# Six h buffers, spread transfers and a seven-product feature group in a gated attention kernel

## The chip, the cores and the metric

The kernel runs on one core of a Trainium2 chip. The metric is the device time of one execution in microseconds (us). The core has five engines that follow their own instruction streams in order and meet through semaphores: TensorE (PE, matmuls, with its weight loads listed as PEld), VectorE (DVE), ScalarE (ACT), GpSimd (POOL) and SyncE (SP), which here only issues transfers. Transfers are also issued from ACT and POOL. A letter q behind an engine's name in a row stands for its sequencer.

## The reference

One layer norm feeds two branches, whose product is added to the input. All data is float32; S = 2048 rows, D = 640, F = 1536.

```python
xn = _layernorm(x, axis=-1)
# A: attention over 8 keys at distance 0, 2, ..., 14; 32 heads of 20
qkv = (xn @ wqkv).reshape(B, S, 3, H, Dh)
idx = pos[:, None] - off[None, :]           # off = arange(8) * 2
logits = where(idx >= 0, einsum("bhsd,bhswd->bhsw", q, k[idx]) * scale, -1e9)
o = einsum("bhsw,bhswd->bhsd", softmax(logits), v[idx])
s = o @ wo
# B: bilinear GLU
h = (xn @ w_gate) * (xn @ w_up)
g = silu(h @ w_down)
out = x + s * g
```

## The kernel before

**Numbers.** Every matmul is done three times on parts: an operand is split into a rounded high part (ACT copy, `split`, line 109) and the low remainder (DVE or POOL subtraction, line 110), and high x high, high x low and low x high are added in PSUM. Splits are thus the constant side work: one ACT and one DVE or POOL instruction for each operand.

**Seven products.** Where it can, the kernel computes a 2x2 block product by seven block products (Strassen's scheme in Winograd's form). It needs sums of blocks on both sides: S1 to S4 (and d5) of the weights, made by `w_add` on POOL (line 1272) and split by `w_split`; T1 to T4 of the normalized, transposed x, kept in `xT` by four chunks of 512 rows. The T blocks of chunks 2 and 3 are made by `differences` (line 1190) during the qkv stage and stay on the chip. Those of chunks 0 and 1 are made early by `early_sums` and `early_high` (lines 583 and 596), stored to `t_scr` and `e_scr`, and loaded back by `load_t` and `load_e` from POOL's queue (lines 1179 and 1184).

**Stages**, in order of time:

1. Up to about 107 us: x is loaded, normalized and transposed; q, k, v of head group 0 and h of features 0 and 1 are computed between. For rows 8 to 15 the moments are spread over partitions by a small matmul (`spread`, line 340) behind a chain of small POOL operations (`scales`). `EARLY` (line 47) says how many of the eight `early_sums` of half 0 are issued ahead of the first `scales`.
2. To 274 us: the qkv projections of the other head groups (`qkv`, line 420). Results go through two or three staging tiles (`staged`: two halves of a slot and one "pk" tile) to `qkv_scr`. The attention runs beside it and goes on into the next stage: a generator (`attention`, line 461) that hands out DVE and POOL work as `advance` gives it credit per matmul. A unit is one head group and one parity of rows; DVE multiplies (527, 498) and reduces (534), POOL adds (504). `ahead` issues loads of q and k (part 0) and v (part 1) on SP.
3. 274 to 512 us: features 2 to 11, 128 each. `group(f, c0)` (line 1287) computes gate and up for two chunks by seven products in order 0, 5, 2, 1, 4, 3, 6, 54 matmuls in all. Products 0, 2, 1 and 4 are copied into an "h" buffer by ACT (`hold`, line 1295, tag "gh", five buffers); the sums `gate_b` (1298), `up_b` (1301), `gate_a` (1308) and the products `h_b` (1304), `up_a` (1311) work in these buffers, which are then stored to `h_scr` from SP. `up_b` and `h_b` stand on DVE for chunks 2 and 3 of features from `VEC` on, otherwise on POOL. Features from `F_TWO` = 3 to 10 take two such groups (chunks 2 and 3, then 0 and 1); feature 2 takes one, and `gate` and `up` (lines 1354 and 1363) for chunks 0 and 1 with 15 plain matmuls each; feature 11 takes one for chunks 0 and 1 and is plain for 2 and 3. The weights' gate part sits in the "pk" tile where a feature is two-way, and `load_wf` brings the next feature's weights.
4. 512 to 597 us: o times wo. Tiles of o come in pairs (`load_pair`), are turned and summed on DVE (`turn_pair`: lines 710 and 982 to 985), split by `hi_pair` on ACT and `lo_pair` on DVE (line 1012), and multiplied (`pair_product`, line 1033); sums and splits of w_down stand between (`wd_sums`, `wd_splits`). Six tiles follow singly.
5. To the end: h times w_down by seven products (line 896), silu, the gating with s and the output.

**Order.** Nothing is scheduled by a planner: each engine's stream is in the order in which the program issues. Two tables place side work behind a product: `places[second, n]` and `beside[f, second, n]`, where n counts the products of a group in issue order. `finish_piece` issues the last gating steps and the stores of a group behind the first product of the next one. Tiles with one tag share that tag's buffers: a new one waits until an old one has been read for the last time.

Of the kernel before, what the change touches and what calls it, by code (L numbers as in the profile page):

```python
# [19 lines left out]
P = 128  # L20
# [25 lines left out]
VEC = 3  # L46
EARLY = 3
# [9 lines left out]
def kernel(  # L57
# [17 lines left out]
    ps = ctx.enter_context(tc.tile_pool(name="ps", bufs=2, space=PSUM))  # L75
    dr = ctx.enter_context(tc.tile_pool(name="dr", bufs=1, space=DRAM))
# [298 lines left out]
    wide, now = [], [None]  # L375
# [44 lines left out]
    def qkv(m, r, i, runs=ALL_RUNS, at=None, act=None, bank=("q", 3)):  # L420
# [9 lines left out]
        if m or r:  # L430
            if not staged:
                y = slot([P, 2, 2 * 3 * CMAX], F32)
                staged.extend([y[:, 0], y[:, 1], st([P, 2 * 3 * CMAX], "pk", 1)])
# [27 lines left out]
    def attention():  # L461
# [45 lines left out]
        for n, u in enumerate(ORDER + [None]):  # L507
            if u is not None:
# [3 lines left out]
                ahead(n, (0, 1))  # L512
# [9 lines left out]
            for j in PAIRS:  # L522
                if u is not None:
                    ahead(n + 1, (0,))
# [20 lines left out]
            ahead(n + 1, (0, 1))  # L545
# [619 lines left out]
    F_TWO = 3  # L1165
# [121 lines left out]
    def group(f, c0=0, second=0):  # L1287
# [26 lines left out]
        if not second:  # L1314
# [65 lines left out]
    def next_sums(f):  # L1380
        w_split(f, "S", "R")
        w_sum.pop(f)
        if f < f1:
            load_wf(f + 1)

    def first_parts():
# [4 lines left out]
        yield  # L1391
        w_split(2, "G")
# [6 lines left out]
    for m, t in ((m, t) for m in range(1, len(MADE)) for t in range(DIL)):  # L1399
# [3 lines left out]
        for i in range(NE):  # L1403
# [9 lines left out]
            qkv(m, r, i)  # L1413
            if i == 1:
# [8 lines left out]
        elif (m, r) == (last, 1):  # L1423
            for k in range(2):
# [6 lines left out]
                   (f0, 1, 4): lambda: sums_wo(), (f0, 1, 5): lambda: split_wo(0, nc.vector),  # L1431
                   (f0, 1, 6): lambda: split_wo(1, nc.vector)})
# [16 lines left out]
    def load_late(n):  # L1449
        if n < 2:  # L1450
            load_t(n + 2)
        else:
            load_e(1, n - 2, n - 2)

    for f in range(2, f1):
        places.clear()
        if not two(f):
            places.update({(0, 3): sums("S1", "S2"), (0, 4): sums("S3", "d5", "S4")})
            if two(f + 1):
                places.update({(0, 0): lambda f: load_t(0), (0, 2): lambda f: load_t(1)})  # L1460
            group(f, 2)
            next_sums(f + 1)
            g0 = gate(f, 0)
            g1 = gate(f, 1)
            if two(f + 1):
                tw.pop("G")
            w_split(f + 1, "G")
# [207 lines left out]
```

## Time and profile before

| | us |
|---|---|
| median of 3 runs | 748.58 |
| lowest and highest | 748.15, 749.75 |
| the profiled execution, its time | 748.28 |
| the profiled execution, its span | 746.5 |
| PE busy | 735.4 |
| DVE busy | 612.2 |
| POOL busy | 462.6 |
| ACT busy | 302.5 |

The span runs from the first to the last instruction of the profiled execution. A row of a timeline has the start and the duration in us, the engine, the line, the operation, what is written and read by the program's names, shapes, and how many instructions are merged in the row; in brackets stands the idle time of the engine just before it and what ended it. A row of a wait list has who waited for whom, the total in us, the number of waits and the longest. Matmuls are pipelined, so the time between the starts of two rows, not their durations, says what a run of matmuls took.

### The profile page before, as it was taken

Reading aid. Unit: us, or ns where it says so; the run is one execution under the profiler, and the core shown is the slowest. Engines: PE = TensorE matmul, PEld = TensorE weight load, DVE = VectorE, ACT = ScalarE, POOL = GpSimd, SP = SyncE. Lnnn points to the kernel's source line nnn. Section 1 sums busy time; section 2 is a strip of 40 time slices with the busy share of each in tenths; the row PEclk is TensorE's granted clock in tenths of the full one; section 3 lists DMA queues with packets and bytes.
Section 4 is the critical chain, followed back from the end, with each engine's and each line's share of the span. In section 5 each row is a group of like instructions: output and inputs, shape, how many; then the busy total and the mean of one; then the engine's idle time right before and its main releaser. Section 6 shows DMA issues by size and latency. Waiting matters only on the chain. (4 is left out here: it accounts for less than half of the span.)

```text
span 746.5 us, 11102 instructions
## 1 busy us (share of the span) xinstructions
PE 735.4 (99%) x4054; PEld 669.0 (90%) x4054; DVE 612.2 (82%) x720; ACT 302.5 (41%) x577; POOL 462.6 (62%) x389
## 2 busy tenths in 40 slices
PE   8999999999999999999999999999999999999997
PEld 6989989988999998778887888887899999999997
DVE  7666998699697887998999999667998777777775
ACT  5658413323332332233223322335556564444442
POOL 6169929787688878888879989877559800000000
PEclk9999999999999999999999999999999999999999
DMA  9465672947446548856165424268567655555534
GB/s 316 170 202 200 236 224 87 299 157 239 127 152 197 190 128 232 274 161 207 55 159 149 115 82 110 72 178 204 167 177 212 228 220 191 191 191 191 191 106 141
DMA packets 103493, 132.98 MB, mean 178 GB/s; under 512 B 22696, under 2 KB 74404, under 8 KB 103438
## 3 DMA queue, kind: packets, MB, share of 16 engines
q1 hardware_dynamic: 84686, 112.77, 48.4%
q10 hardware_dynamic: 17600, 14.26, 5.9%
q0 software_dynamic: 1152, 5.24, 2.2%
q8 instruction: 32, 0.52, 0.3%
q14 instruction: 23, 0.19, 0.1%
HBM read 83.58 MB, written 47.81 MB: 176 GB/s over the span
## 5 line engine op out<-in xcount | busy, mean ns | idle before, releaser
L504 POOL TENSOR_TENSOR o<-o,t 128x960 f32<-128x960 f32 (+1 forms) x69 | 139.6, 2024 | 19.1 <-DVE t L498 17.6
L498 DVE TENSOR_TENSOR t<-e,kv 128x960 f32<-128x960 f32 (+1 forms) x96 | 99.4, 1037 | 24.8 <-POOL o L504 24.7
L527 DVE TENSOR_TENSOR t<-q,kv 128x1920 f32<-128x1920 f32 (+1 forms) x48 | 92.4, 1925 | 4.3 <-DMA kv<-qkv_scr 4.2
L534 DVE TENSOR_REDUCE lg<-t 128x96 f32<-128x1920 f32 (+1 forms) x48 | 92.3, 1922 | 0.2
L428 PE MATMUL q<-s,xc 128*128 128x360 f32 (+1 forms) x450 | 83.1, 334 | 0.6 <-DVE lg L266 0.5
L110 POOL TENSOR_TENSOR s<-wraw,s 128x384 fp32r<-128x384 f32 (+6 forms) x58 | 69.6, 1210 | 19.9 <-ACT s L109 19.9
L428 PEld LDWEIGHTS q<-s,xc 128*128 128x128 f32 x450 | 74.9, 188 | 4.8 <-DVE lg L266 0.8
L1295 ACT ACTIVATE gh<-g 128x512 f32<-128x512 f32 x54 | 32.2, 597 | 115.8 <-PE g L1328 97.8
L428 PE MATMUL u<-s,xc 128*128 128x360 f32 (+1 forms) x360 | 65.8, 334 | 0.0
L428 PEld LDWEIGHTS u<-s,xc 128*128 128x128 f32 x360 | 60.3, 188 | 2.3
L428 PE MATMUL g<-s,xc 128*128 128x360 f32 (+1 forms) x330 | 61.5, 337 | 0.0
L428 PEld LDWEIGHTS g<-s,xc 128*128 128x128 f32 x330 | 55.7, 188 | 2.6
L1328 PE MATMUL u<-xc,s 128*128 128x512 f32 x216 | 55.3, 391 | 0.9 <-ACT gh L1295 0.9
L896 PE MATMUL q<-xc,s 128*128 128x320 f32 x342 | 55.5, 309 | 0.0
L1328 PE MATMUL g<-s,s 128*128 128x512 f32 x216 | 55.0, 390 | 0.0
L896 PEld LDWEIGHTS q<-xc,s 128*128 128x128 f32 x342 | 51.5, 188 | 0.0
L1328 PEld LDWEIGHTS u<-xc,s 128*128 128x128 f32 x216 | 40.3, 188 | 10.5 <-ACT gh L1295 2.0
L1328 PEld LDWEIGHTS g<-s,s 128*128 128x128 f32 x216 | 40.5, 188 | 8.6 <-ACT gh L1295 0.2
L109 ACT ACTIVATE s<-wraw 128x384 fp32r<-128x384 f32 (+6 forms) x59 | 33.5, 587 | 29.5 <-PE g L1328 9.0
L504 POOL TENSOR_TENSOR o<-t 128x960 f32<-128x960 f32 (+1 forms) x12 | 24.4, 2032 | 31.8 <-DVE t L498 25.2
L1328 PE MATMUL g<-xc,s 128*128 128x512 f32 x168 | 41.5, 391 | 1.3 <-ACT gh L1295 1.3
L119 PE MATMUL g<-xc,s 128*128 128x512 f32 (+1 forms) x180 | 40.1, 373 | 0.0
(367 smaller groups left out, 1566.5 us busy)
## 6 DMA issues: line engine op xcount, KB each, us to landing
h_scr<-gh SPq DMA_DIRECT2D x48, 256.0 KB, 2.6
wraw<-in_wgu SPq DMA_DIRECT2D x11, 640.0 KB, 4.4
kv<-qkv_scr SPq DMA_DIRECT2D x14, 480.0 KB, 5.9
qkv_scr<-s ACTq DMA_DIRECT2D x18, 360.0 KB, 4.4
t<-h_scr SPq DMA_DIRECT2D x8, 768.0 KB, 7.1
kv<-qkv_scr SPq DMA_DIRECT2D x14, 367.5 KB, 6.6
s_scr<-gh SPq DMA_DIRECT2D x16, 320.0 KB, 4.2
gh<-s_scr SPq DMA_DIRECT2D x16, 320.0 KB, 3.5
```

The lines of the kernel that those rows point to most:

```text
L109: nc.scalar.activation(hi, raw, AF.Copy)
L110: eng.tensor_sub(lo, raw, hi.bitcast(F32))
L119: nc.tensor.matmul(acc, a, b, start=first and n == 0, stop=last and n == len(runs) - 1)
L428: nc.tensor.matmul(p, xT[(r * NE + i) // TPC][a][:, k, t0:t0 + P], wq[m][b][k], start=n == 0, stop=n == len(runs) - 1, skip_group_check=ac ...
L498: nc.vector.tensor_mul(t.rearrange("p (n d) -> p n d", d=DH), e[:, :, w].unsqueeze(2).to_broadcast([P, NE * nh, DH]), v)
L504: return NE * c * cost, lambda: eng.tensor_add(y, z, t)
L527: nc.vector.tensor_mul(t, q, k)
L534: nc.vector.tensor_reduce(out=lg[:, :, j:j + 2].rearrange("p n a -> p a n"), in_=t.rearrange("p a (n d) -> p a n d", d=DH), op=ALU.add, ax ...
L896: nc.tensor.matmul(p, y[:, i, k], wd_t[name][k][:, l], start=new and r == 0, stop=r == len(runs) - 1, skip_group_check=True)
L1295: nc.scalar.activation(kept[j], b["ACACABA"[j]], AF.Copy)
L1328: nc.tensor.matmul(y, w, x, start=j in (0, 1, 5) and r == 0, stop=r == len(runs) - 1, skip_group_check=True)
```

## The change

It has these parts. `F_TWO` becomes 2: feature 2 takes two groups of seven products, so its gate weights go to the "pk" tile (the staging of the last qkv products gives that tile up), its up weights shrink to three blocks, the sums of feature 3's weights take the places that later features use, and all loads of T and e blocks of chunks 0 and 1 come a feature earlier. `VEC` becomes 2 with it. `EARLY` becomes 1. The "gh" tag gets a pool of its own with six buffers, which is closed ahead of the pairs and followed by one of five. `load_wf` moves from the start of a group behind its first product. In `attention` the loads of v move from the end of the unit before to the third key of their own unit, and those of q and k behind that. The stores of q, k, v of head group 0 go from ACT's queue to SP's. On the way to the o pairs, `split_wo(0)`, `split_wo(1)` and `turn_pair(0)` come one or two products later, and `turn_pair(2)` goes from between the last gate and up to behind product 5 of pair 0.

```diff
-VEC = 3
-EARLY = 3
+VEC = 2
+EARLY = 1
...
+    halfway = ExitStack()
+    gh_pool = [halfway.enter_context(tc.tile_pool(name="six", bufs=1)), 6]
...
-        return sb.tile(shape, dt, tag=tag, bufs=bufs, name=f"{tag}_{cnt[0]}")
+        pool = sb
+        if tag == "gh":
+            pool, bufs = gh_pool
+        return pool.tile(shape, dt, tag=tag, bufs=bufs, name=f"{tag}_{cnt[0]}")
...
-                    nc.scalar.dma_start(scr[2 * g + r][:, :, i - 1:i + 1, :], y[:, k])
+                    (nc.scalar if m else nc.sync).dma_start(scr[2 * g + r][:, :, i - 1:i + 1, :], y[:, k])
...
-                ahead(n, (0, 1))
+                ahead(n, (0, 1) if late_unit else (0,))
...
             for j in PAIRS:
                 if u is not None:
-                    ahead(n + 1, (0,))
+                    if j == 2:
+                        ahead(n, (1,))
+                    elif j > 2:
+                        ahead(n + 1, (0,))
...
-            ahead(n + 1, (0, 1))
+            ahead(n + 1, (0,))
...
-    F_TWO = 3
+    F_TWO = 2
...
             wf_raw.pop(f)
-            if f < f1 and f + 1 not in wf_raw:
-                load_wf(f + 1)
...
+            if (second, n) == (0, 0) and f < f1 and f + 1 not in wf_raw:
+                load_wf(f + 1)
             advance(PACE * len(runs) * (GROUP_RATE if two(f) else 0.184))
...
         w_split(2, "S")
-        yield
-        w_split(2, "G")
         yield
...
             qkv(m, r, i)
+            if m == last and n == NT - 7:
+                staged[:] = [y for y in staged if y is not stage_pk[-1]]
+            elif m == last and n == NT - 5:
+                load_t(0)
+            elif m == last and n == NT - 3:
+                w_split(2, "G")
...
-                   (f0, 1, 4): lambda: sums_wo(), (f0, 1, 5): lambda: split_wo(0, nc.vector),
-                   (f0, 1, 6): lambda: split_wo(1, nc.vector)})
+                   (f0, 1, 4): lambda: sums_wo(), (f0, 1, 6): lambda: split_wo(0, nc.vector)})
...
     def load_late(n):
-        if n < 2:
-            load_t(n + 2)
+        if n == 0:
+            load_t(1)
+            load_t(2)
+        elif n == 1:
+            load_t(3)
         else:
-            load_e(1, n - 2, n - 2)
+            load_e(1, 0, 0)
+            load_e(1, 1, 1)
...
         places.update(two_places)
         if f == F_TWO:
-            places.update({(0, n): lambda f, n=n: load_late(n) for n in range(4)})
+            for n in range(3):
+                places[0, n] = lambda f, n=n: load_late(n)
         group(f, 2)
         group(f, 0, 1)
     places.clear()
-    beside.update({(f1, 0, 0): lambda: (turn_pair(0), load_pair(1)), (f1, 0, 4): lambda: (hi_pair(0, 0), lo_pair(0, 0)),
+    beside.update({(f1, 0, 0): lambda: split_wo(1, nc.vector),
+                   (f1, 0, 2): lambda: (turn_pair(0), load_pair(1)), (f1, 0, 4): lambda: (hi_pair(0, 0), lo_pair(0, 0)),
...
     g3 = gate(f1, 3)
-    turn_pair(2)
     up(f1, 3, g3)
...
     pair_k.append(st([P, 3, HALF], "o", 1))
+    halfway.close()
+    gh_pool[:] = [ctx.enter_context(tc.tile_pool(name="five", bufs=1)), 5]
...
         if p == 0:
             load_pair(4)
+            turn_pair(2)
```

The branch of the loop for a feature that is not two-way (its `places`, `next_sums`, `gate` and `up` for chunks 0 and 1) falls away.

More of the change, by code (lines that the diff above doesn't have):

```diff
@@ L1378, in up @@
         advance(PACE * 2.8)
[L1380 to L1384, printed above, removed]
     def first_parts():
@@ L1449, in load_late @@
     def load_late(n):
-        if n < 2:
-            load_t(n + 2)
-        else:
-            load_e(1, n - 2, n - 2)
+        if n == 0:
[3 more added lines that the diff above has]
+            load_t(3)
+        else:
+            load_e(1, 0, 0)
+            load_e(1, 1, 1)
     for f in range(2, f1):
         places.clear()
[L1457 to L1467, printed above, removed]
-            up(f, 0, g0)
-            up(f, 1, g1)
-            if two(f + 1):
-                tw.pop("U")
-            continue
         places.update(two_places)
         if f == F_TWO:
-            places.update({(0, n): lambda f, n=n: load_late(n) for n in range(4)})
+            for n in range(3):
+                places[0, n] = lambda f, n=n: load_late(n)
         group(f, 2)
```

5 lines of the change are left out of this document (3 added, 2 removed).

## The prediction

> **What bounds the kernel now.** I read the page first, then the list of who waited for whom with TensorE (PE) as the one that waits, with the total, the number of waits and the longest, then a table of busy time by stretch.
>
> ```profile
> span 746.5 us, 11102 instructions
> PE 735.4 (99%) x4054; PEld 669.0 (90%) x4054; DVE 612.2 (82%) x720; ACT 302.5 (41%) x577; POOL 462.6 (62%) x389
> ```
>
> ```profile
> PE g L1328 <- ACT gh L1295: 1.3, 2, 0.9
> PE e L340 <- POOL lg L334: 1.0, 1, 1.0
> PE u L1328 <- ACT gh L1295: 0.9, 2, 0.6
> PE e L1033 <- DVE xc L1012: 0.8, 1, 0.8
> ```
>
> ```profile
> 273.90:299.70 25.80, 25.80 (x116) 21.40 (x115) 20.13 (x24) 8.53 (x15) 22.60 (x21) 1.00 0.82 230
> 299.70:472.60 172.90, 171.17 (x749) 139.74 (x749) 162.22 (x160) 54.36 (x91) 147.69 (x114) 1.00 0.49 140
> 525.80:566.00 40.20, 39.10 (x262) 38.28 (x261) 37.09 (x60) 24.60 (x54) 22.68 (x20) 1.00 0.58 163
> ```
>
> The columns of the table are the stretch, its length, then PE, weight loads, DVE, ACT, POOL, the granted clock, DMA share and GB/s. PE is busy in all but 11.1 us of the span and is the bound in every stage, so only two things shorten the kernel: fewer matmuls, or fewer of its holes. The waits list names the holes one by one, and each has a place in the change. The table gives the warning: in the feature groups DVE is busy 162.22 of 172.90 us, in the output pairs 37.09 of 40.20. It is the next bound, close behind.
>
> **Part 1, feature group 2: fewer matmuls.**
>
> ```profile
> 273.90 1.52 PE L1328 MATMUL g<-xc,s 128*128 128x512 f32 x6
> ...
> 286.14 3.56 PE L119 MATMUL g<-xc,s 128*128 128x512 f32 x15
> ...
> 299.74 1.90 PE L1328 MATMUL g<-xc,pk 128*128 128x512 f32 x6
> 301.48 2.21 PE L1328 MATMUL q<-xc,pk 128*128 128x512 f32 x9
> ...
> 299.29 1.56 POOL L110 TENSOR_TENSOR pk<-wraw,pk 128x640 fp32r<-128x640 f32 x1
> ```
>
> From 273.90 to 286.14 chunks 2 and 3 go by seven products: 54 matmuls in 12.24 us, 0.2267 each. From 286.14 to 299.74 chunks 0 and 1 go by plain gate and up: 60 matmuls in 13.60. The second becomes a second 54, so **-1.36 us**, six matmuls by 0.2267. Then the first product of group 3 takes 1.74 us where six take 1.36: the gate weights were split too late (POOL at 299.29, the product at 299.74). With group 2 as a two-way group these weights are split five products ahead, as in the later groups: **-0.38**.
>
> What it adds. POOL gets the up sum and h product of chunks 0 and 1 and gives those of chunks 2 and 3 to DVE; DVE also gets the two gate sums and a product in place of two plain products. The nearest row for the sums and the product on DVE is this one:
>
> ```profile
> L1304 DVE TENSOR_TENSOR gh<-gh,gh x8: 679/1000/2370, 314.8 to 490.1; 128x512 f32<-128x512 f32 x8
> ```
>
> Two more on DVE are 1.4 to 4.7 us, the two gate sums about as much as the two products that go. The stretch of group 2 has 5.67 us of idle DVE to take it, so I cost it at nothing; with that cover gone it would be the same 1.4 to 4.7 us at most. The Trainium skill (SBUF — State Buffer, "Who interferes with whom") has a rule that speaks against this step: a VectorE instruction with two SBUF inputs and a GpSimd instruction that reads SBUF exclude each other for a whole instruction. The spread from 679 to 2370 ns agrees; by the rule DVE falls behind whenever POOL is full, which is the first rival below.
>
> The T blocks, the sums of x for chunks 0 and 1, must also be in a group earlier. Block 0 is issued five qkv products before the group, 1 and 2 behind its first product, 3 behind the second, the two e blocks behind the third, all on POOL.
>
> ```profile
> 279.93 0.76 POOL L1182 DMA_DIRECT2D s<-t_scr  x1
> ...
> DMA to landing us min/median/max: 8.8/10.6/11.7
> ```
>
> At 279.93 POOL stood at the place where blocks 1 and 2 will now be issued. They are needed 15 matmuls into the second half, at 286.14 + 3.40 = 289.54. With the shortest landing block 1 is there at 288.7 and block 2 just behind: no stall. With the longest it lands at 291.6 and block 2, 768 KB at the 230 GB/s of the stretch, 3.4 us later: at most 5.5 us at that product, and 6.7 when the e blocks, 2.3 us each behind block 3, hold the last product too. Ends 0 and 6.7; I take **+0.6**, near the short end, because the key loads of the attention that ran beside them move away and block 0 is already in. The Trainium skill (DMA: Bandwidth & Descriptors, "Anatomy of one DMA — SWDGE (gpsimd) path") puts such a transfer at 2.0 us plus bytes over 436e3 per us, an estimate of 3.8 us for 768 KB. The trace has 8.8 to 11.7, and the trace decides; by the page's figure this term would be 0.
>
> The gate split of group 2 (1.56 us on POOL) and the issue of block 0 (0.76) now stand among the attention's last sums of the qkv stage, ahead of the R and U splits that products three and four want: ends 0 and 2.3. I take 0: the same split leaves POOL's queue a few products earlier, in front of the same sums, and U shrinks from five blocks to three. The q, k, v staging does without its third tile for the last products; each of the two others still has a pair of products in which its store can land: 0.
>
> **Part 2, EARLY 3 to 1.**
>
> ```profile
> 44.84 3.59 PE L119 MATMUL g<-xc,s 128*128 128x512 f32 x15
> 49.46 0.41 PE L340 MATMUL e<-lg,lg 128*128 128x32 f32 x2 [1.03 <-POOL lg L334]
> ...
> 43.79 2.55 POOL L593 TENSOR_TENSOR kv<-xc 128x512 f32<-128x512 f32 x2 [17.92 <-DVE xc L370]
> ...
> 47.55 0.21 POOL L278 TENSOR_TENSOR lg<-lg 128x4 f32<-128x4 f32 x1
> ...
> 45.02 0.17 DVE L277 RECIPROCAL lg<-lg 128x4 f32<-128x4 f32 x1
> ```
>
> The product of 15 ends at 44.84 + 15 x 0.2267 = 48.24; the spread starts at 49.46, so the hole is 1.22. It waits for the scales chain on POOL, which starts at 47.55 behind three early sums and ends just before 49.46. With one early sum ahead POOL is free at 45.1 and the reciprocal is there at 45.2: the chain starts 2.3 us earlier. **-1.22**. Two sums move behind the second scales and end later; their stores and, on SP, the stores of unit 1's q, k and v queue behind them. What waits for those is the attention, by the loads that come next, not a product: 0.
>
> **Part 3, six buffers of h and the spread transfers.**
>
> ```profile
> 320.86 2.20 PE L1328 MATMUL u<-xc,s 128*128 128x512 f32 x9
> 323.53 2.35 PE L1328 MATMUL g<-xc,s 128*128 128x512 f32 x9 [0.47 <-ACT gh L1295]
> ...
> 332.52 1.52 PE L1328 MATMUL g<-s,s 128*128 128x512 f32 x6
> 334.34 2.35 PE L1328 MATMUL u<-xc,s 128*128 128x512 f32 x9 [0.30 <-ACT gh L1295]
> ...
> 395.82 2.20 PE L1328 MATMUL u<-xc,s 128*128 128x512 f32 x9
> 398.90 2.34 PE L1328 MATMUL g<-xc,s 128*128 128x512 f32 x9 [0.87 <-ACT gh L1295]
> ...
> 505.89 1.52 PE L1328 MATMUL g<-s,s 128*128 128x512 f32 x6
> 508.01 2.34 PE L1328 MATMUL u<-xc,s 128*128 128x512 f32 x9 [0.60 <-ACT gh L1295]
> ```
>
> ```profile
> ACT gh L1295 <- DMA h_scr<-gh: 12.3, 4, 6.9
> ```
>
> Against 0.2267 each the four holes are 0.63, 0.46, 1.04 and 0.76: 2.89. Each ends when ACT's copy of a product into an h buffer is done, and that copy had waited for a buffer: the one before it was still being stored. A sixth buffer gives every copy one store more of time. The stores also start sooner: they no longer stand on SP behind the next group's weight load nor, at a unit's end, behind loads of k and v that wait for DVE; the weight load comes a product later, four ahead of the sums that read it, and the v load two steps into its own unit, a unit ahead of its use: 0 each. What is late next is DVE's gating, which the sixth buffer covers too. Between keeping all four holes (0) and losing them all I take **-2.89**.
>
> **Part 4, o pairs.**
>
> ```profile
> 531.10 1.48 PE L1033 MATMUL g<-s,kv 128*128 128x320 f32 x9
> 532.42 0.75 PE L1033 MATMUL e<-s,xc 128*128 128x320 f32 x4
> 533.96 0.56 PE L1033 MATMUL e<-s,xc 128*128 128x320 f32 x2 [0.78 <-DVE xc L1012]
> 534.75 1.15 PE L1033 MATMUL q<-xc,kv 128*128 128x320 f32 x6 [0.23 <-DVE gh L1042]
> ...
> 536.18 1.04 PE L1033 MATMUL u<-xc,s 128*128 128x320 f32 x6
> 537.30 1.14 PE L1033 MATMUL e<-xc,s 128*128 128x320 f32 x6
> ...
> 527.73 1.56 DVE L710 STREAM_TRANSPOSE s<-s 128x640 f32<-128x640 f32 x2
> ...
> 532.41 1.50 DVE L1012 TENSOR_TENSOR xc<-s,xc 128x640 fp32r<-128x640 f32 x1
> ```
>
> Here a matmul takes (532.42 - 531.10) / 9 = 0.147. From 532.42 to 534.75 six stand: 1.45 too long. Nine to 536.18 are 0.11 too long, six to 537.30 0.24. Together 1.80. The low part that PE waits for (532.41) stands on DVE behind the turning of pair 2 from 527.73 on, some 3.2 us. That step moves behind product 5 of pair 0, where nothing waits for it before pair 2. So the low part comes 3.2 us sooner and the holes go: **-1.80**. But DVE, full to 37.09 of 40.20, must do the step between two pairs: ends 0 and 1.80 again. The five h buffers of the second half also start there, over the six, and DVE's first sum into one may wait for the last h store. I take **+0.4** for both, near the low end, because the pairs' stretch has 3.1 us of idle DVE, about one turning. The same order ahead of group 11 (gate sums before the turning of pair 0) shortens the last hole of part 3 and is counted there.
>
> **Sum.** -1.36 - 0.38 + 0.6 - 1.22 - 2.89 - 1.80 + 0.4 = -6.65. The profiled execution took 748.28 us, its span 746.5, so it would be 741.63. The median of the runs shown, 748.58, is 0.30 above it: **741.9**.
>
> **The rivals.** *DVE becomes the bound.* For it: 162.22 of 172.90 busy, and PE gives back some 3 us of that stretch while up to 4.7 come in. Against: 10.7 us of it are idle, and six buffers let gating lag. The holes of part 3 then come back as waits for gating, two thirds of them: 741.9 + 1.9 = 743.8.
>
> *The hole of the pairs only moves.* Pair 2 is turned between the high parts of pair 1 and its own, and PE waits at pair 2 as it did at pair 1: the 1.80 comes back, 743.7, or twice that if pair 3 follows late, 745.5. Against: the low part of pair 2 is needed some 8 us later than that of pair 1.
>
> *The T blocks come late, and the kernel is slower.* POOL is busy 22.60 of 25.80 in this stretch, and the gate split and block 0 stand ahead. If POOL reaches blocks 1 and 2 three us later than 279.93 and landing takes the longest, 11.7, block 2 lands at 298.0 and the second e block near 306, against 296.3 where the last product wants it: 9.7 us of hole, 741.9 - 0.6 + 9.7 = 751. It turns the sign once block 2 lands later than about 297. For it: longest landing seen under just such traffic. Against: less runs beside them now, and block 0 is out of their way.
>
> *The sixth buffer does nothing,* because the copies wait for stores that come no earlier: part 3 falls out, 744.8. The wait row, which names the store itself, speaks against it.
>
> **How the numbers follow.** The forecast has 0.58, DVE 0.13, the moved hole 0.09, the idle sixth buffer 0.07, the late blocks 0.13, of which 0.09 above 750.1 and 0.04 near no change. The range starts at 739.8: without the two added terms the sum gives 740.9, and after a hole nine matmuls take 2.35 us where they take 2.20 at 320.86, 0.15 more for each of seven holes. It ends at 746.5 and leaves out little but the late blocks. A measurement of this kernel can tell about 0.2%, 1.5 us, from no change. Below 747.1 lie the first four cases, 0.87, of which I take 0.03 off for two of them at once: faster 0.84, within 0.07, slower 0.09.
>
> **What would show it.** Right: 54 matmuls in the second half of group 2; the spread for rows 8 to 11 starts as its gate product ends; no wait of PE for ACT's gh copies; none for L1012 in the first pairs. Wrong: PE waiting for a T block at the third product of group 2's second half, copies still waiting for h stores, or DVE with no idle time between 300 and 470 and PE holes behind its gate sums.

## The result and the profile after

The changed kernel takes 745.4 us (median of 5 runs, 744.77 to 745.68). The kernel before, run beside it, took 748.95 us (748.15 to 750.33). The ratio is 0.9948, with a 95% interval of 0.9933 to 0.9962. So the kernel is faster, and inside the range of 739.8 to 746.5, but it gained about half of the 6.65 us of the sum: 3.55 us by the medians, 2.88 between the two profiled executions.

The profiled execution took 745.40 us against 748.28 before. Here are the line of its page on the engines, and the list of what PE waited for from the start of group 2 to the first products of the last stage. Lines of the code are five to nine higher than before: 1335 is the product of a group, 1304 the copy into an h buffer, 1313 the product h. In the pairs 1042 is the product, 1045 ACT's copy of a product, 1048, 1051 and 1053 are the sums on DVE and 1021 the low parts. 510 is a sum of the attention, 115 a split's subtraction, 905 a product of the last stage.

```profile
PE 734.1 (99%) x4048; PEld 668.4 (90%) x4048; DVE 620.4 (83%) x723; ACT 303.0 (41%) x579; POOL 464.0 (62%) x389
```

```profile
PE u L1335 <- POOL s L115: 1.1, 1, 1.1
PE q L1042 <- DVE gh L1051: 0.9, 1, 0.9
PE e L1042 <- DVE gh L1051: 0.4, 1, 0.4
PE e L1042 <- ACT o L1045: 0.4, 1, 0.4
PE u L905 <- ACT s L864: 0.2, 1, 0.2
PE g L1335 <- ACT gh L1304: 0.2, 1, 0.2
```

Six matmuls are gone, as forecast, and PE is busy 1.3 us less. The waits for ACT's copies, 2.2 us before, are down to 0.2. But two names stand here that did not stand there: a weight split on POOL, and sums on DVE in the pairs. The same shows in the table by stretch (columns as before: stretch, length, PE, weight loads, DVE, ACT, POOL, granted clock, DMA share, GB/s):

```profile
272.40:296.90 24.50, 24.50 (x110) 20.33 (x109) 23.27 (x30) 8.87 (x16) 23.10 (x23) 1.00 0.99 295
296.90:468.80 171.90, 171.75 (x755) 141.21 (x755) 162.14 (x155) 55.68 (x93) 147.14 (x112) 1.00 0.44 129
468.80:493.30 24.50, 23.40 (x104) 19.03 (x103) 16.15 (x17) 6.77 (x12) 20.20 (x15) 1.00 0.46 134
521.17:562.96 41.79, 39.85 (x262) 38.27 (x261) 38.69 (x60) 24.53 (x54) 23.55 (x21) 1.00 0.59 160
```

In group 2 the added sums have used up most of DVE's idle time, from 5.67 to 1.23 us, and PE has no hole there. Features 3 to 9 run almost without a hole (171.75 of 171.90). Feature 10 loses 1.1 us. The pairs, 40.17 us long before, take 41.79, and DVE is busy 38.69 us in them, against 37.06 before.

A ledger, read from the starts of PE's rows in the two profiled executions:

| stretch | before | after | measured | forecast |
|---|---|---|---|---|
| to the first product of group 2 | 273.90 | 272.47 | -1.43 | -1.22 |
| group 2 | 25.84 | 24.48 | -1.36 | -1.36, +0.6 for the T blocks |
| group 3 to the first plain product of feature 11 | 212.49 | 210.51 | -1.98 | -0.38 and -2.89 |
| plain products of feature 11 | 13.60 | 13.71 | +0.11 | 0 |
| the pairs | 40.17 | 41.79 | +1.62 | -1.80 and +0.4 |
| single tiles of o | 27.72 | 27.73 | +0.01 | 0 |
| last stage, to the last matmul | 148.07 | 148.43 | +0.36 | 0 |
| sum | | | -2.67 | -6.65 |

**Where parts 1 and 2 gained.** The second half of group 2 is now 54 matmuls, and nothing in it waits. The columns of a timeline are start, duration, engine and line, tiles and count.

```profile
284.71 1.52 PE L1335 MATMUL g<-xc,pk 128*128 128x512 f32 x6
...
288.11 1.52 PE L1335 MATMUL g<-s,s 128*128 128x512 f32 x6
...
296.95 1.52 PE L1335 MATMUL g<-xc,pk 128*128 128x512 f32 x6
```

```profile
L1191 POOL DMA_DIRECT2D s<-t_scr x4: 537/557/758, 264.1 to 279.1; - x4
...
DMA to landing us min/median/max: 5.6/8.6/11.0
```

The second block of rows sums up the T blocks' loads. They land in 5.6 to 11.0 us. Block 2 is the one that counts: it landed at 287.97, and the product that reads it began at 288.11. The margin is narrow. In the run with five buffers below the same load landed at 288.16, and the third matmul of that product, due at 288.10, began at 288.20.

```profile
44.70 3.59 PE L124 MATMUL g<-xc,s 128*128 128x512 f32 x15
48.13 0.30 PE L345 MATMUL e<-lg,lg 128*128 128x32 f32 x2
```

The spread's small matmuls now start as the product of 15 ends (44.70 + 15 x 0.2267 = 48.10); the wait of 1.03 us for POOL is gone.

**What is new at 477 us.** Two timelines, of PE and POOL:

```profile
475.44 0.61 PE L1335 MATMUL u<-xc,s 128*128 128x512 f32 x2
477.16 0.50 PE L1335 MATMUL u<-xc,s 128*128 128x512 f32 x1 [1.10 <-POOL s L115]
```

```profile
471.73 2.25 POOL L510 TENSOR_TENSOR o<-o,t 128x960 f32<-128x960 f32 x1
473.94 1.29 POOL L1310 TENSOR_TENSOR gh<-gh,gh 128x512 f32<-128x512 f32 x1
475.19 1.91 POOL L115 TENSOR_TENSOR s<-wraw,s 128x384 fp32r<-128x384 f32 x1
```

The low parts of feature 10's up weights (475.19) stand on POOL behind a sum of the last attention unit and an up sum. They end at 477.10, and the third matmul of the product that reads them starts then, 1.27 us late, with 0.11 more on the next matmul. DVE had been idle for 2.21 us, up to 474.02.

**What is new in the pairs.** PE and DVE at the first pair:

```profile
527.77 1.04 PE L1042 MATMUL e<-s,xc 128*128 128x320 f32 x6
529.67 1.14 PE L1042 MATMUL q<-xc,kv 128*128 128x320 f32 x6 [0.86 <-DVE gh L1051]
```

```profile
526.14 0.81 DVE L1021 TENSOR_TENSOR xc<-s,xc 128x640 fp32r<-128x640 f32 x1
528.73 0.49 DVE L1048 TENSOR_TENSOR gh<-o,u 128x320 f32<-128x320 f32 x1 [1.77 <-POOL kv L115]
529.13 0.48 DVE L1051 TENSOR_TENSOR gh<-o,q 128x320 f32<-128x320 f32 x1
```

DVE sits idle for 1.77 us before its first sum into one of the five new buffers (528.73), and the second sum, which PE needs, stands behind it. The view names a POOL split as the releaser, which ended at 528.54. The last store of h, issued at 525.89, landed at 528.44, so either could be it. Further on DVE has 0.09 us of idle time at two places and no more up to 559 us, and a hole of 0.3 to 0.5 us, with 0.1 on the next matmul, stands in each pair.

Which DVE rows grew? Mostly the four low parts of 128x768. Here is the second of them, before and after:

```profile
540.26 0.95 DVE L1012 TENSOR_TENSOR kv<-s,kv 128x768 fp32r<-128x768 f32 x1
```

```profile
536.67 1.46 DVE L1021 TENSOR_TENSOR kv<-s,kv 128x768 fp32r<-128x768 f32 x1
```

Before, all four began as a POOL split ended or ahead of one, and took 0.94 to 0.95 us. After, three of the four begin 0.24 to 0.42 us into a POOL split of 0.88 us, and take 1.27 to 1.46. That is 1.3 of the 1.6 us by which DVE is busier.

### The profile page after: what moved, and what is told of

It reads as the page before. It is cut to its first block, busy times and chain, and to the rows that moved or that the text cites. A ratio compares the mean times of both kernels' runs of the same rounds, so it can differ in the third digit from the quotient of the medians.

```text
span 743.6 us, 11095 instructions
## 1 busy us (share of the span) xinstructions
PE 734.1 (99%) x4048; PEld 668.4 (90%) x4048; DVE 620.4 (83%) x723; ACT 303.0 (41%) x579; POOL 464.0 (62%) x389
## 5 line engine op out<-in xcount | busy, mean ns | idle before, releaser
L1304 ACT ACTIVATE gh<-g 128x512 f32<-128x512 f32 x57 | 34.1, 598 | 113.2 <-PE g L1335 110.1
L1335 PE MATMUL u<-xc,s 128*128 128x512 f32 x228 | 58.4, 390 | 1.1 <-POOL s L115 1.1
L1335 PE MATMUL g<-s,s 128*128 128x512 f32 x228 | 58.1, 390 | 0.0
L1335 PEld LDWEIGHTS u<-xc,s 128*128 128x128 f32 x228 | 42.8, 188 | 10.9 <-POOL s L115 1.9
L1335 PEld LDWEIGHTS g<-s,s 128*128 128x128 f32 x228 | 42.7, 188 | 9.2 <-ACT gh L1304 0.4
L1335 PE MATMUL q<-xc,pk 128*128 128x512 f32 x171 | 41.8, 389 | 0.0
```

The source lines that it names most:

```text
L1304: nc.scalar.activation(kept[j], b["ACACABA"[j]], AF.Copy)
L1335: nc.tensor.matmul(y, w, x, start=j in (0, 1, 5) and r == 0, stop=r == len(runs) - 1, skip_group_check=True)
```

## The experiments

All runs change the kernel after, unless said otherwise. "Groups to end" is the time from the first product of group 2 to the end of the last matmul in the profiled execution (before: 467.89, after: 466.65). It is given because the stages ahead of it vary: in the executions profiled of two of the kernels below (own space for the last h, and two amendments) they took 2.6 to 2.8 us longer than in the kernel after, with the same code. So a difference of the medians of less than about 1 us is not put down to an edit by itself; the trace of the place has to show it.

| run | median us | ratio to before, interval | groups to end |
|---|---|---|---|
| five buffers | 746.36 | 0.9968, 0.9956 to 0.9980 | 467.74 |
| turn put back | 745.07 | 0.9953, 0.9939 to 0.9968 | 466.72 |
| own space for the last h | 743.53 | 0.9939, 0.9923 to 0.9955 | 465.63 |
| up weights on DVE | 744.58 | 0.9946, 0.9933 to 0.9959 | 465.40 |
| own space, sums first | 744.37 | 0.9948, 0.9936 to 0.9961 | 464.83 |
| loads not spread | 748.72 | 1.0006, 0.9993 to 1.0019 | 467.07 |
| the same, another execution | 749.17 (one run) | | 470.82 |
| three amendments | 743.30 | 0.9930, 0.9918 to 0.9942 | 464.91 |
| EARLY = 3 | 746.18 | 0.9963, 0.9949 to 0.9976 | 466.37 |
| two amendments | 743.73 | 0.9937, 0.9921 to 0.9953 | 464.42 |
| sums on POOL | 744.22 | 0.9950, 0.9934 to 0.9966 | 464.75 |
| sums left out | 740.89 | 0.9906, 0.9878 to 0.9935 | 461.49 |

### Part 3: the buffer and the spread, one at a time

```diff
-    gh_pool = [halfway.enter_context(tc.tile_pool(name="six", bufs=1)), 6]
+    gh_pool = [halfway.enter_context(tc.tile_pool(name="six", bufs=1)), 5]
```

> The changed kernel with five buffers of h in the feature groups instead of six; the spread transfers and all else stay. If the sixth buffer is what closed the holes of before at 323.53, 334.34, 398.90 and 508.01 us (0.63, 0.46, 1.04 and 0.76, together 2.89 us), those holes are back and the time is about 745.4 + 2.9 = 748.3 us. If the transfers that were spread over a group did it, the time stays within 0.5 us of 745.4 and no group of products gets longer. In either case the five-buffer pool of the pairs still starts where the earlier pool ends, so the first hole of the pairs (1.02 us at 529.67) should stay, shifted with the stage.

Between the two. The groups, 234.76 us from their first to their last product in the kernel after, take 236.40, so the sixth buffer is worth 1.64 us there and about 1 us in the median. The holes that are back are at other places. PE, ACT and POOL of this run:

```profile
405.41 0.96 PE L1335 MATMUL u<-xc,s 128*128 128x512 f32 x3 [1.27 <-ACT gh L1304]
```

```profile
404.76 0.60 ACT L1304 ACTIVATE gh<-u 128x512 f32<-128x512 f32 x1 [3.30 <-POOL gh L1313]
```

```profile
401.21 2.27 POOL L510 TENSOR_TENSOR o<-o,t 128x960 f32<-128x960 f32 x1
403.42 1.30 POOL L1313 TENSOR_TENSOR gh<-gh,gh 128x512 f32<-128x512 f32 x1
```

The buffer is late because POOL forms the product h (403.42) behind a sum of the attention (401.21). Was that new? These are ACT's copies ahead of three of the four holes of the kernel before, those at 334.34, 398.90 and 508.01 us (1295 and 1304 are there what 1304 and 1313 are after):

```profile
333.69 0.60 ACT L1295 ACTIVATE gh<-u 128x512 f32<-128x512 f32 x1 [2.33 <-POOL gh L1304]
398.25 0.60 ACT L1295 ACTIVATE gh<-g 128x512 f32<-128x512 f32 x1 [2.98 <-DMA h_scr<-gh]
507.36 0.60 ACT L1295 ACTIVATE gh<-u 128x512 f32<-128x512 f32 x1 [2.63 <-POOL gh L1304]
```

It was not: two of them waited for POOL's product h, and only one for a store. (At 323.53 the view names a product of PE.) The waits of these copies for stores were 12.3 us before and are 2.6 here, with five buffers and the spread loads; those for the product h were 8.3 us and are 10.0.

There is no hole at 477 us in this run. The likely reading, which no run tests apart, is that POOL had caught up by then, with 1.55 us lost at 405 and 1.07 at 455: the sixth buffer lets PE run ahead, and POOL's debt shows later. The gross worth of the buffer would then be 1.64 + 1.38 = 3.0 us, its net worth 1.64. The wait at the start of the pairs stayed (0.99 us), as expected.

The other half of part 3, with the six buffers kept:

```diff
-                ahead(n, (0, 1) if late_unit else (0,))
+                ahead(n, (0, 1))
...
-                    if j == 2:
-                        ahead(n, (1,))
-                    elif j > 2:
-                        ahead(n + 1, (0,))
+                    ahead(n + 1, (0,))
...
-            ahead(n + 1, (0,))
+            ahead(n + 1, (0, 1))
```

> The changed kernel with six buffers of h, but attention's loads ahead placed as before (both blocks of the next unit asked for together, one further at each pair of keys), so that only the sixth buffer is tested. If the sixth buffer alone closed the holes, the feature groups stay within 0.5 us of the changed kernel's (239.7 us from the first product of group 2, at 272.47, to the pairs less the plain products: 234.76 us to the last product of the groups at 507.23) and the time within 0.5 us of 745.4. If the spread of the transfers carries part of it, holes on gating come back in the groups in which they were before (about 324, 334, 399 us), 0.4 to 1.1 us each, and the time is 746 to 748 us.

The second theory holds in its time, but not for its reason. The median of 12 runs is back at the time of before, yet the gating holes at 324, 334 and 399 us do not return: with six buffers the copies do not wait for stores even without the spread. There is one new hole: the third product of group 2's second half waits 1.51 us for T block 2. The execution that was profiled was the fastest of the twelve, so another one was profiled.

> The same kernel as in the run with attention's loads placed as before, for the trace of another execution: the one that was profiled was the fastest of its twelve (746.16 us against a median of 748.72) and showed one hole that the changed kernel has not, 1.51 us on the landing of the second T block at 290.16 us. If that wait is what varies, this execution, if it is slower, has a longer hole at the same place, and the T blocks land later than 286.0, 290.1 and 292.5 us. If the time is lost elsewhere, that hole stays near 1.5 us and another place shows it.

The hole is longer, 2.15 us, and something worse stands behind it. PE of this run (line 1332 is 1335 of the kernel after), then the stretch behind the wait:

```profile
290.32 1.54 PE L1332 MATMUL g<-s,s 128*128 128x512 f32 x4 [1.99 <-DMA s<-t_scr]
291.66 2.76 PE L1332 MATMUL u<-s,s 128*128 128x512 f32 x6
```

```profile
290.32:294.22 3.90, 3.90 (x11) 3.02 (x12) 3.90 (x5) 1.22 (x2) 0.97 (x1) 0.59 1.10 372
```

The granted clock falls to 0.59 for the 3.9 us behind the wait, and six matmuls that take 1.36 us elsewhere take 2.56 (291.66 to 294.22). In all, group 2 takes 28.39 us, 3.9 more than in the kernel after. The T blocks were issued as early as there, block 2 at 278.19; it landed at 290.27, not 287.97. Why it was late shows on SP's queue, first of the kernel after, then of this run:

```profile
277.61 0.39 SPq L419 DMA_DIRECT2D kv<-qkv_scr  x1
278.05 1.18 SPq L421 DMA_DIRECT2D kv<-qkv_scr  x2
...
288.97 0.34 SPq L413 DMA_DIRECT2D q<-qkv_scr  x1
```

```profile
277.20 0.39 SPq L413 DMA_DIRECT2D q<-qkv_scr  x1
277.95 0.32 SPq L419 DMA_DIRECT2D kv<-qkv_scr  x1
278.33 1.83 SPq L421 DMA_DIRECT2D kv<-qkv_scr  x2
```

Unspread, the three loads of v are out by 275 and the four of the next unit's q and k go beside the T blocks. Spread, only the three of v go beside them, and q and k follow from 288.97 on, when the blocks have nearly landed. So what the spread buys is not time for gating but room for the T blocks, and it is what lets part 1 have its gain: 748.72 - 745.4 = 3.3 us in the medians. The two traces, 0.42 and 4.17 us longer from group 2 to the end, lie on both sides of that.

### Part 2: EARLY back to 3

> The changed kernel with three early sums instead of one ahead of the scales of the third block (EARLY = 3). If the scales were late because GpSimd formed those sums first, the spread's matmuls wait again at about 48.2 us for GpSimd, the feature groups start 1.2 us later (273.7 instead of 272.47 us), nothing later takes it back, and the time is about 746.6 us. If the wait is hidden by something else, the time stays within 0.3 us of 745.4.

The first theory. The wait is back, the groups start at 273.64, 1.17 us later than in the kernel after, and what comes behind takes about as long (466.37 us against 466.65). The median is 0.8 us longer, not 1.2.

```profile
49.19 0.41 PE L345 MATMUL e<-lg,lg 128*128 128x32 f32 x2 [1.10 <-POOL lg L339]
```

### The hole at 477 us: POOL's queue

```diff
-            split(nc.gpsimd, y, tw[to][:, 0, r], tw[to][:, 1, r])
+            split(nc.vector if (f, t) == (10, "U") else nc.gpsimd, y, tw[to][:, 0, r], tw[to][:, 1, r])
```

> The changed kernel with the low parts of feature group 10's up weights formed on VectorE instead of GpSimd. Theory A (the hole of 1.27 + 0.11 us at 477.16 us is GpSimd's queue: this subtraction stands behind an attention sum and the up sum and ends at 477.10, while VectorE was idle for 2.21 us just before): the hole goes, nothing else gets late, and the time is near 744.0 us. Theory B (attention's last unit as a whole is late): another wait on VectorE or GpSimd takes its place within the same group, and the time stays within 0.4 us of 745.4.

The first theory. The products of this group follow each other without a hole, feature 11's plain products start at 505.67 instead of 507.46 (0.24 of that is an earlier start of group 2), and groups to end is 1.25 us shorter. On DVE the step takes 0.55 us where POOL took 1.91. The timed runs (744.58) lean the same way without separating the two.

### The pairs: handover, order, or work

```diff
-            hs = st([P, CH], "gh", 5)
+            hs = st([P, CH], "gh", 5) if (f, ch) != (f1, NCH - 1) else st([P, CH], "pk", 1)
```

> The changed kernel with the last h product written into the space of the gate weights (tag pk) instead of a buffer of h, so that VectorE's first sum into the new five buffers doesn't wait for the last store of h (landed 528.44, the sum started 528.73 after 1.77 us idle). Theory A (the handover is an extra loss by itself): the sum starts near 527.0, the hole at 529.67 (1.02 + 0.10 us) goes, and the time is near 744.3 us. Theory B (VectorE is full anyhow and only moves its lateness to the next product 6): the first hole goes, but those at 532 to 560 grow by as much, and the time stays within 0.3 us of 745.4.

The first theory for the first hole. The products run through where PE had waited. Timelines of DVE and of POOL, then the pairs in the table:

```profile
530.25 0.48 DVE L1048 TENSOR_TENSOR gh<-o,u 128x320 f32<-128x320 f32 x1
...
531.05 0.95 DVE L1021 TENSOR_TENSOR s<-t,s 128x768 fp32r<-128x768 f32 x1
```

```profile
531.03 1.70 POOL L115 TENSOR_TENSOR kv<-wraw,kv 128x320 fp32r<-128x320 f32 x1
```

```profile
524.58:565.16 40.58, 39.58 (x262) 38.26 (x261) 39.25 (x60) 24.54 (x54) 24.91 (x21) 1.00 0.60 165
```

The pairs are 1.21 us shorter, and the later holes are as they were. The first sum (530.25) now begins without a wait, 0.78 us ahead of the POOL split that the view had named, and ahead of the landing of the last h store at 531.44. So the releaser was that store, not the split. What stays is 40.58, still 0.4 above the kernel before.

```diff
+    turn_pair(2)
     up(f1, 3, g3)
...
-            turn_pair(2)
```

> The changed kernel with the turn of the third o pair put back ahead of the last up product. Theory A (VectorE is full in the pairs: 38.69 of 41.80 us busy, against 38.3 us of matmuls without their holes): about 3.4 us of VectorE work leave the pairs, the holes from 532 us on (0.25, 0.53, 0.28, 0.29, 0.53 and their follow-ups) go, the pairs take about 39.5 us instead of 41.79, and the time is near 743.3 us. Theory B (the move was right, and only the handover between the two pools of h costs): the hole of before at the start of the pairs comes back on top of the handover, and the time is 746.5 us or more.

Both are right for one half. The holes behind the first pair are gone, all of them. But the one of the kernel before is back and larger, and the clock falls behind it:

```profile
530.16 0.56 PE L1042 MATMUL e<-s,xc 128*128 128x320 f32 x2 [1.70 <-DVE xc L1021]
```

```profile
531.00:534.20 3.20, 3.20 (x12) 3.20 (x13) 2.71 (x5) 0.83 (x2) 0.00 (x0) 0.51 0.14 51
```

PE waits for the same low part as in the kernel before, 1.87 us against 0.95 there, and then pays 0.12 us more for each matmul of a dozen: the pairs take 42.18. So the turn of pair 2 costs PE at either place, once as one large hole or in each pair as a small one.

```diff
-            if p:
-                lo_pair(p + 1, 2)
             hi_pair(p + 1, 1)
         pair_product(p, 4)
         wd_splits()
-        if not p:
-            lo_pair(1, 2)
         if more:
+            lo_pair(p + 1, 2)
             lo_pair(p + 1, 1)
```

> As the run before with the last h product in a space of its own, and in the pairs VectorE's fourth sum (the one product 6 waits for) goes ahead of the low part of the next pair's sums, which is now formed behind product 4. Theory A (what is left in the pairs is the order on VectorE: the fourth sum stands behind a low part that takes 1.45 us while GpSimd splits beside it): the holes of 0.53, 0.28 and 0.29 us (and 0.1 behind each) at 541, 549 and 557 us go, the pairs take about 39.2 us instead of 40.58, and the time is near 742.4 us. Theory B (VectorE is simply full): the low parts are late instead, product 0 to 2 of the next pair wait as long, and the pairs stay at 40.4 to 40.8 us.

The second theory: 40.71 us. The holes do not go, they move from product 6 to product 2 of the next pair, which waits for ACT's copy of product 0, and the copy for DVE's last sum of the pair before. With feature 10's weights on DVE as well:

> The changed kernel with all three amendments: the last h product in a space of its own (1.2 us in its run's trace), the up weights' low parts of feature group 10 on VectorE (1.4 us in its run's trace), the fourth sum of each pair ahead of the low part. If the three stages are independent, the gains add: 745.4 - 1.2 - 1.4 - 1.4 = about 741.4 us, with the pairs at about 39.2 us and no hole at 477 us. If VectorE is the bound behind them, one gives back what another brings, and the time is 742.5 us or more.

The second case in its time, 743.30 us. The hole at 477 us is gone and the groups take 1.0 us less than in the run before, but the pairs take 41.41, 0.7 more than without that step. All of the 0.7 stands at one place in the first pair, the same that was shown above for the own space alone. DVE and POOL of this run:

```profile
526.68 1.68 DVE L1021 TENSOR_TENSOR s<-t,s 128x768 fp32r<-128x768 f32 x1
```

```profile
526.66 0.88 POOL L115 TENSOR_TENSOR kv<-wraw,kv 128x320 fp32r<-128x320 f32 x1
```

The two start within 0.02 us of each other in both runs. With the own space alone (531.05 and 531.03) DVE's took 0.95 us and POOL's 1.70; here it is 1.68 and 0.88. DVE's last sum of the pair, ACT's copy behind it and product 2 of the next pair then come late. So the 0.7 us is which of the two went first. The same without the new order of sums:

> The changed kernel with two amendments: the last h product in a space of its own and the up weights' low parts of feature group 10 on VectorE; the order of the sums in the pairs stays the change's. If the two are independent, 745.4 - 1.2 - 1.4 = 742.8 us, with no hole at 477 us and the pairs at 40.6 us. If the stage ahead arrives earlier and VectorE and GpSimd are then later against it, part is given back in the pairs: they take 41.2 us or more, and the time is 743.3 us or more.

Again the second in its time: 743.73 us, the pairs at 41.32, 0.74 more than with the own space alone. It is the same again: the low part takes 1.68 us and the split 0.87 at that place, PE has a hole of 0.89 us behind them instead of 0.17, and all other holes of the pairs agree within 0.01. So this is not DVE being late against an earlier PE, as the expectation had it. The two meet like this in six of the runs here. POOL went first in these two; DVE went first in the two without feature 10's low parts on DVE and in the two below that have them. What decides it is not shown.

Of the versions that compute the whole, the lowest medians are 743.30 and 743.73 of these two and 743.53 of the own space alone, some 2 us under the kernel after. The intervals of their ratios still touch that of the kernel after, and do not rank the three. Next, part of DVE's work is given to POOL:

```diff
-        nc.vector.tensor_add(s1, a21, a22)
-        nc.vector.tensor_sub(s2, s1, a11)
-        nc.vector.tensor_sub(s4, a12, s2)
-        nc.vector.tensor_sub(a21, a11, a21)
+        eng = nc.gpsimd if p > 1 else nc.vector
+        eng.tensor_add(s1, a21, a22)
+        eng.tensor_sub(s2, s1, a11)
+        eng.tensor_sub(s4, a12, s2)
+        eng.tensor_sub(a21, a11, a21)
```

> As the kernel with the two amendments, and the four sums behind the turn of o pairs 2, 3 and 4 (4 x 0.43 us each on VectorE) go to GpSimd, which is idle there for 3.6 to 7 us in each pair. Theory A (VectorE is the bound of the pairs: about 38.7 us of work in a stage whose matmuls need 38.3 us): the pairs take 39.4 us or less, and the time is 1 us or more under the kernel with the two amendments alone. Theory B (the bound is VectorE and GpSimd together, since either takes longer while the other runs): VectorE's remaining work gets longer or GpSimd's splits come late, and the pairs take as long as there, within 0.3 us, or longer.

The second theory. And last, the same sums left out:

```diff
+        if p < 2:
```

> The kernel with the two amendments (last h product in its own space, feature group 10's low parts on VectorE), but the four sums behind the turn of o pairs 2, 3 and 4 are left out: these pairs multiply unsummed parts. Theory A (work on VectorE itself is the bound of the pairs): 12 x 0.43 = 5.2 us of it are gone, its first sums follow each other at the pitch of 54 matmuls (54 x 0.147 = 7.9 us) instead of 8.1 to 8.5 us, the holes behind pair 1 shrink to 0.2 us each, and the pairs take about 39.3 us instead of 41.3. Theory B (the bound is the order, the one buffer in which the products 0 to 2 are kept and the sum that reads it last): the holes of 0.53, 0.29, 0.29 and 0.54 us stay within 0.15 us, and the pairs take over 40.8 us.

The first theory, clearly (this kernel leaves out work that the result needs). The pairs of the last three runs, in this order, the first and the last with the group of three of their low parts (line 1022 is 1021 of the others):

```profile
522.35:563.67 41.32, 39.59 (x263) 38.28 (x261) 39.99 (x60) 24.51 (x54) 24.21 (x21) 1.00 0.60 163
```

```profile
L1021 DVE TENSOR_TENSOR s<-t,s x3: 1274/1453/1676, 528.8 to 554.0; 128x768 fp32r<-128x768 f32 x3
```

```profile
519.20:561.21 42.01, 39.80 (x263) 38.28 (x261) 37.97 (x48) 24.52 (x54) 34.26 (x33) 1.00 0.56 154
```

```profile
519.39:557.93 38.54, 38.54 (x262) 38.27 (x261) 33.98 (x48) 24.49 (x54) 24.57 (x21) 1.00 0.61 170
```

```profile
L1022 DVE TENSOR_TENSOR s<-t,s x3: 946/949/949, 525.9 to 548.5; 128x768 fp32r<-128x768 f32 x3
```

With 12 sums out of the stage altogether, DVE is busy 6.0 us less and the pairs take 38.54 us, which is their matmuls and one hole of 0.16 + 0.10. The sums themselves were 5.1 us of that, and the same low parts take 0.949 us where they took 1.453: each now begins ahead of a POOL split or goes first. With the 12 sums on POOL, DVE is busy only 2.0 us less, POOL 10.1 us more, and the pairs get longer, not shorter. In both runs DVE went first at the place in the first pair, so the fair comparison is with the 40.58 us of the own space alone: 2.0 us shorter without the sums, 1.4 longer with them on POOL. The Trainium skill (SBUF — State Buffer, "Who interferes with whom") says that a DVE instruction with two inputs in SBUF, the on-chip memory, and a POOL instruction that reads SBUF exclude each other. The rows agree: 0.95 and 1.70 us, or 1.68 and 0.88, for the same two. It is the work of DVE and POOL together that holds PE here, and neither the other order of sums nor the exchange tried above helps.

## Why the prediction was right or wrong

The direction and the range were right. That the time lies in the range is partly luck: losses of 3.0 and 1.4 us that the sum did not have were cushioned by 0.6 us for late blocks that were not late. By its own steps:

**Part 1, right, and for a reason that it gave no weight.** Group 2 lost 1.36 us to the hundredth, without the stall for which +0.6 was added. Against the range of 0 to 6.7 that looks like luck, but the runs without the spread show what decided it: block 2 lands 2.2 to 2.3 us later, the stall is 1.5 to 2.2 us, and with the fallen clock group 2 loses up to 3.9. The forecast did say that key loads "move away" from beside the blocks, as a reason for the short end. It booked the gain of that in part 1 as a small thing and costed the spread itself under part 3. The spread belongs to part 1 almost wholly. The rival that T blocks come late was thus a real danger, at the right place, that another edit of the same change had taken away by a narrow margin. Where the prediction has the sign turn once block 2 lands later than about 297 us, its own chain through the e blocks gives about 295.6; with the landing at 287.97 nothing hung on it. The 0.38 came as forecast: the six matmuls from 296.95 take 1.36 us instead of 1.74.

**Part 2, right.** 1.22 forecast, 1.43 in the trace, 1.17 with EARLY put back. The start of the groups varies by some tenths from run to run; the hole itself went from 1.22 to 0.03.

**Part 3, right in what it removes, wrong in the wait and in that nothing follows.** All four holes are gone, and the rival that the sixth buffer does nothing is out. But the reading that each copy had waited for a store does not hold: the row of 12.3 us has four waits, and only one of them (2.98 us at 398.25) stands ahead of one of the four holes; two stood behind POOL's product h. A buffer more helps against either wait, so the number came out. The step that failed is "What is late next is DVE's gating, which the sixth buffer covers too". What is late next is POOL: its product h holds the buffers when there are only five, and with six its weight split holds PE at 477 us for 1.27 + 0.11. Without that hole group 3 and what follows would have gained 1.98 + 1.38 = 3.36, against 3.27 forecast. The profile of before had POOL busy 147.69 of 172.90 us in these groups, less full than DVE, and the forecast looked at DVE alone.

**Part 4, wrong: a gain of 1.40 forecast, a loss of 1.62 measured.** The old hole behind the low part did go. The step that failed is the +0.4 for the two things put in its place, taken near the low end of 0 to 1.80. They cost 1.80 + 1.62 = 3.4 us in all: 1.21 the wait of the first sum for the last h store, the other 2.2 DVE in the pairs. Both things had been named. The end of 1.80 was too short, since it let the old hole come back only once, and the handover had no price of its own. The reason for the low end, "the pairs' stretch has 3.1 us of idle DVE, about one turning", does not hold. Of the 3.1 us DVE spent 2.4 waiting for ACT's high parts and for a product, and the turn, at 527.73, already lay inside that stretch, so the room was never what mattered. DVE does the same instructions there before and after; it is busy 1.63 us longer, 1.3 of it because three low parts now begin inside a POOL split where they had begun ahead of one. The rival "the hole of the pairs only moves" came nearest: DVE's lateness did come back. But it had PE wait at pair 2 for the low part, as before; the holes stand in every pair, at product 6 behind a sum, and the handover is not in it. That 745.4 lies in its 743.7 to 745.5 is chance, since 1.4 us of the loss are at 477. The last stage's 0.36 (a wait for ACT at 593.66) is no effect of the change: in eleven of the twelve runs above that stage takes 148.0 to 148.2 us with the same code.

So the sum is off by 6.65 - 2.67 = 4.0 us in the traces: 3.0 in the pairs and 1.4 at 477 us, less 0.6 for the blocks that were not late, and some tenths besides.

## What to carry to other kernels

Idle time of an engine in a stage is not room for more work: where it stands behind the engine's inputs, or where a neighbour's instructions lengthen its own, one step moved in can show up as a hole in each iteration. So test a full stage by leaving work out before shuffling its order. Before two versions of such a stage are ranked, see whether two instructions that start together went in the same order in both: here that was worth 0.7 us. A row of a wait list is a sum: match each of its waits to the hole that it is said to make. When buffers or spread loads let the bound engine run ahead, look for the next queue that it will outrun, on every engine, and at the places where one pool of buffers ends and another begins over the same memory. And read an edit's worth where it acts: transfers that are moved pay for those that they no longer meet, which may be another part's.

## What the runs showed of the hardware

**A short wait can cost most of its length again.** Behind PE waits of 1.70 and 1.99 us the granted clock fell to 0.51 over 3.2 us and to 0.59 over 3.9 us, and the matmuls there took about 1.5 us more in all. Behind the wait of 1.35 us in the first execution with the unspread loads, that of 1.10 at 477 us and one of 1.39 at 477.06 with the turn put back, the matmuls kept their pace. The Trainium skill (TensorE: Matmul & The Clock Gate, "What's actually happening") has the clock halved after an idle window of about 3.4 us; the rows here show it after a wait of about half that length. What the limit is, and whether it depends on when the wait begins, these waits can't tell.

**Two that exclude each other.** A DVE subtraction of 128x768 and a POOL split that began within 0.02 us of each other took 0.95 and 1.70 us when DVE went first, 1.68 and 0.88 when POOL did. Begun 0.24 to 0.42 us into a split, such a subtraction took 1.27 to 1.46. Which of two goes first can differ between kernels that differ elsewhere.
